# Free time behind list-scheduled operations and a new opening for a one-core transformer block

## The chip, the cores and the metric

The kernel runs on one core of a Trainium2 chip. A core has four compute engines that the profile names PE (TensorE, matrix products), DVE (VectorE), ACT (ScalarE) and POOL (GpSimd), and SP (SyncE), which issues most DMA transfers. Each engine takes its instructions in the order in which the program lists them; an instruction that waits for a semaphore holds everything behind it on its engine. The metric is device time in microseconds. Three runs of the kernel before took 972.73 to 976.04 us, with a median of 974.53.

## The reference

The kernel computes one transformer block with adaptive layer norm for a sequence of 2048 tokens of width 512. A conditioning vector gives six vectors of 512 (scale, shift and gate for each half of the block). Attention has 32 heads of 16 and a causal sliding window of 256; the FFN is SwiGLU with 1792 hidden units. All data are 32-bit floats.

```python
mod = (_silu(c) @ w_mod).reshape(c.shape[0], 6, 1, -1)
sa, ca, ga, sb, cb, gb = (mod[:, 0], mod[:, 1], mod[:, 2], mod[:, 3], mod[:, 4], mod[:, 5])
h = _layernorm(x, axis=-1) * (1 + ca) + sa
x = x + ga * _A_ref(h, A_wqkv, A_wo)          # windowed attention and out-projection
h = _layernorm(x, axis=-1) * (1 + cb) + sb
x = x + gb * _B_ref(h, B_w1, B_w3, B_w2)      # w2 (silu(w1 h) * (w3 h))
```

## The kernel before

A product in 32-bit precision is made from parts: an operand is split into a rounded part of type fp32r and the rest (a copy with rounding, and a subtraction), and three matmuls of 512 columns add up high by high, low by high and high by low. So a copy and a subtraction stand in front of nearly every matrix product: `wvh` and `wvl` for the value weights, `wq` (two parts) for the query and key weights, `hT` (two parts) for the normed and transposed input, `wo` and `o` for the out-projection, `w` for the FFN weights, `b` for FFN inputs.

The work falls into three stretches.

The opening (to about 90 us) loads x, the modulation weights and the value weights, makes rows of the modulation (`modulation`: four matmuls `row` on PE, a copy `out` to ACT, a turn into columns `turn` on PE, and `end` on DVE, which writes `modc`), the statistics and the normalization of the first 512 tokens (`ln1`: statistics on DVE, the power on POOL, `ln_apply` on DVE, transposes on PE, then for each of four 128-wide slices an ACT copy `h` with scale and shift, and the pair of DVE operations in `mod_split` that writes `hT`), the value products (`values`, tile `st`) and the first query and key products (`unit_a`, tile `pj`). Each function hands its operations with a time to `at(t, fn)`; they are sorted by that time and issued in this order. The times are offsets in the dictionaries W (opening) and Y (first units). They are a planner's units of order, not measured times. Before, a few set-up operations stood outside this list: masks and identity copies on DVE, the copy `sc32` of the conditioning vector, and the first `ring_fill`, which puts constants into the buffers (`ring`) of queries and keys; the fills of the other three token blocks were in the list, and POOL did them.

Attention runs as 32 units, 8 groups of four heads by 4 blocks of 512 tokens. A unit has a part a (query and key products, `pj`, with splitting), a part b (row maxima: score matmuls `mx` on PE, then a DVE operation L507 with the mask that leaves the maximum `mt`, then `mr` and a small matmul L522), and a part c (scores `st` again, exp on ACT to `pt`, window selects on POOL (L778) or DVE, products with the values `po`, L726). The order of these operations is written out by hand in the dictionary X.

From the last third of the units on, a list scheduler, class `Sched`, puts other work between the unit operations: loading and splitting of wo and of the FFN weights (`split`, L962 copy and L963 subtraction), the reciprocals of the softmax sums (L1065), the attention outputs multiplied by the reciprocals and split (`o_part`: L1095, L1087, L1090), the out-projection with the residual (`o_proj`, matmuls L1107, DVE L978), the second layer norm (L983 to L1003, L1228), its transposes (L1242) and splitting (L1246 to L1267), and the whole FFN. The FFN's block products are formed from sums and differences of blocks, seven products instead of eight, so DVE and POOL also form sums of tiles. The unit operations enter as `fixed`, with a time and an engine. `deal` goes forward in planned time: for each engine it takes the first operation by key whose inputs are ready, or else the one that is ready first, and picks the earliest over all engines; a fixed operation goes in when its time has come. Keys, and for many operations the engine, stand in the dictionary K; CAPS limits how many PSUM banks each use may hold.

Of the kernel before, what the change touches and what calls it, by code (L numbers as in the profile page):

```python
# [18 lines left out]
P = 128  # L19
# [24 lines left out]
W = dict(m=0.15, s=0.1, a=0.32, t=0.541, p=0.377, vs=1.762, vo=0.422, wq=-2.02, ws=-0.376, wv0=-1.811, wv=0.3, wvk=0.474, h0=0.539, h=6, hb=6.874, ls=3.287, la=1.146, rf=7.313, v=2, vt=1.75, m0=1.5, mt=0.7, ml=0.241, A=1.268, At=7.876, B=9.889)  # L44
# [22 lines left out]
CAPS = dict(tp=4, up=5, dn=5)  # L67
# [47 lines left out]
class Sched:  # L115
# [38 lines left out]
    def deal(self):  # L154
# [8 lines left out]
        order, self.dealt = [], []  # L163

# [102 lines left out]
LATE = 2.0  # L267

# [5 lines left out]
def us(t):  # L274
# [15 lines left out]
K = dict(be=(('POOL', 'POOL'), ('POOL', 'DVE'), ('POOL', 'POOL'), ('DVE', 'POOL'), ('POOL',  # L290
         'POOL'), ('POOL', 'DVE'), ('POOL', 'POOL')), hr=1.228, de=-0.011, wo=0.363, x1=5.427,
         xb=-11.259, xl=0.182, os=0.09, ol=(-29.26, -4.358, -61.448, -4.772), pl=(23.674, -19.281,
         -2.126, -37.597), pe=(1.308, 32.004, -0.229, 9.552), o=(-92.491, -1.503, 76.848, -7.065),
         n=(1, 1, 2, 2), w0=0.298, l2=0.646, f=3.115, fl=5.405, by=((('POOL', 'POOL'), ('POOL',
         'POOL'), ('DVE', 'DVE'), ('POOL', 'POOL')), (('POOL', 'POOL'), ('POOL', 'DVE'), ('DVE',
         'DVE'), ('POOL', 'POOL')), (('POOL', 'DVE'), ('DVE', 'DVE'), ('DVE', 'DVE'), ('DVE',
         'DVE')), (('POOL', 'POOL'), ('DVE', 'DVE'), ('DVE', 'DVE'), ('DVE', 'POOL'))), w=0.25,
         dn=1.72, ds=0.103, l3=-4.114, sw=('POOL', 'DVE', 'DVE', 'POOL'), su=(('POOL', 'DVE',
         'DVE', 'POOL'), ('POOL', 'POOL', 'POOL', 'DVE'), ('DVE', 'DVE', 'DVE', 'POOL')),
         sr=(('POOL', 'DVE', 'DVE', 'DVE', 'POOL', 'DVE', 'DVE', 'DVE', 'DVE', 'DVE', 'DVE'),  # L300
         ('POOL', 'DVE', 'POOL', 'DVE', 'POOL', 'DVE', 'DVE', 'POOL', 'DVE', 'POOL', 'POOL')))
@with_exitstack
def block_kernel(ctx: ExitStack, tc: tile.TileContext, x, wqk, wv, wo, w13, w2, c, wmod, out):
# [13 lines left out]
    for hh in range(2):  # L317
        r = slice(64 * hh, 64 * hh + 64)
        nc.vector.tensor_reduce(
            out=odd[r], in_=ident[r].rearrange("p (c o) -> p c o", o=4)[:, :, 2 - 2 * hh:4 - 2 * hh],  # L320
            op=ALU.add, axis=mybir.AxisListType.XY)
# [85 lines left out]
    nc.vector.tensor_scalar(later, mskk[:, 0], 0.0, None, op0=ALU.is_lt)  # L407
    mskr = ap.tile([P, 2, P], F32R, name="mskr")
    nc.vector.tensor_copy(mskr, mskk)
    mskk = mskr.bitcast(F32)  # L410
    identr = ap.tile([P, P], F32R, name="identr")
    nc.vector.tensor_copy(identr, ident)

    def ring_fill(b):
        for hh in range(2):
            k = ring.bitcast(F32)[:, 2 - 2 * hh, :, b * BT:(b + 1) * BT]
            eng = nc.vector if b == 0 and hh == 0 else nc.gpsimd
            eng.memset(k[:NM] if hh == 0 else k[:NS], 0.0)
            if hh:
                eng.memset(k[NS:NM], 1.0)  # L420
            eng.memset(k[NS:NS + 2], 1.0 - hh)
# [3 lines left out]
    def load_wqk(g, n):  # L425
# [144 lines left out]
    nc.vector.tensor_copy(sc32, sc[:, :, None].to_broadcast([P, KC, 32]))  # L570

    def modulation(j, s, t0, at):
# [14 lines left out]
        def out():  # L587
            v["e"] = p0.tile([P, D], F32, name="h32", bufs=3)
            nc.scalar.activation(v["e"], v[0], AF.Copy)
# [19 lines left out]
        for n, fn in enumerate((row, out, turn, end)):  # L609
            at(t0 + W["m"] * n, fn)  # L610

# [3 lines left out]
    def load_wv(k, n):  # L615
# [3 lines left out]
        elif n == 1:  # L619
            nc.scalar.activation(wvh[:, k], raw, AF.Copy)  # L620
        else:
            nc.gpsimd.tensor_tensor(out=wvl[:, k], in0=raw, in1=wvh.bitcast(F32)[:, k],
                                    op=ALU.subtract)
# [59 lines left out]
    ring_fill(0)  # L683
    h0 = -40.0
    modulation(0, 2, h0 - 1, at)
    modulation(1, 1, h0 - 0.9, at)
    for n in range(3):
        at(h0 + (W["wq"] if n == 0 else W["ws"] + n * 0.02), lambda n=n: load_wqk(0, n))
# [13 lines left out]
    m0 = v0 + W["vt"] * W["m0"]  # L702
    for n, (j, s) in enumerate(((3, 2), (4, 1), (2, 2), (5, 1))):
        t = v0 + W["vt"] * (W["m0"] + W["mt"] * n)
        at(h0 + W["ml"] if n < 2 else t - 2 * W["vt"] * W["mt"] + W["m"] * 0.5, lambda j=j, s=s: load_mod(j, s, nc.sync))
        modulation(j, s, t, at)
    at(v0 + W["vt"] * (W["m0"] + W["mt"] * 3) + 3.1 * W["m"], ones)
    for u in range(3):
        unit_a(u, h0 + W["A"] + W["At"] * u, at, Y)
# [891 lines left out]
```

## Time and profile before

| | before |
|---|---|
| median of three runs | 974.53 us (972.73 to 976.04) |
| profiled execution | 973.01 us |
| its span, first to last instruction | 971.3 us |
| mean granted TensorE clock | 0.99 |
| PE busy | 940.5 us |
| DVE, ACT, POOL busy | 743.1, 556.4, 542.8 us |

The profiled execution is one of its own; it lies 1.52 us below the median of the three. In rows of the trace the first number is the start, the second the time from the first start to the last end of a run of equal instructions, then engine, source line, operation, the tile written and the tiles read. Brackets at the end give the idle time of the engine before the row, and what released it. Half a clock means that a matmul of the same size takes twice as long. PE takes weights (PEld) ahead of the matmul that uses them. Rows can be shown overlapping, since the matmuls are pipelined and other engines start the next operation before the last has wholly ended.

### The profile page before, as it was taken

To read this page: it belongs to the slowest core of one execution; us is meant where nothing else is said; L and a number is where in the kernel's file an instruction comes from. 1 tells how busy PE (TensorE), PEld (TensorE's weight loads), DVE (VectorE), ACT (ScalarE), POOL (GpSimd) and SP (SyncE) were. 2 spreads that over 40 slices of the span, in tenths; PEclk is the share of its full clock that TensorE was granted. 3 is DMA by queue.
4 is the path that set the end of the run, shared out by engine and by line. 5 is a ranking of instruction groups with operands and counts; after the bars stand their busy time and mean duration, and the time that the engine had idled before them with its cause. 6 is when DMAs were issued, how large, how long until landed. Compare 5 with 4: busy or idle time off the path is not lost.

```text
span 971.3 us, 17147 instructions
## 1 busy us (share of the span) xinstructions
PE 940.5 (97%) x5316; PEld 716.7 (74%) x5316; DVE 743.1 (77%) x2032; ACT 556.4 (57%) x1252; POOL 542.8 (56%) x742
## 2 busy tenths in 40 slices
PE   5999999999999999998898999999999999999998
PEld 3578777777777776774577888888887888888886
DVE  7776799899989898999378686656679765677545
ACT  3433787787878787876578843433456343423330
POOL 7441787877777776765556765347759332222320
PEclk9999999999999999999799999999999999999999
DMA  8521354444454444335695564467654432222102
GB/s 294 182 88 34 118 175 153 143 160 139 146 178 143 144 144 143 133 122 180 211 237 145 188 225 149 142 206 249 188 199 166 141 119 89 69 62 75 44 23 87
DMA packets 80672, 141.65 MB, mean 146 GB/s; under 512 B 9538, under 2 KB 22338, under 8 KB 80580
## 3 DMA queue, kind: packets, MB, share of 16 engines
q1 hardware_dynamic: 79860, 139.50, 44.6%
q10 hardware_dynamic: 720, 1.05, 0.3%
q8 instruction: 42, 0.69, 0.3%
q14 instruction: 50, 0.41, 0.1%
HBM read 85.72 MB, written 34.61 MB: 124 GB/s over the span
## 4 chain that ended last, share of the span: by engine, by line
PE 83%; POOL 5%; DVE 5%; DMA 2%; issue 2%; ACT 1%; SPq 1%; POOLq 0%; DVEq 0%; ACTq 0%
PE st L1371 13%; PE mx L1371 11%; PE mx L500 7%; PE pj L447 7%; PE mx L1465 7%; PE st L750 7%; PE st L1465 7%; PE po L726 6%; PE pj L1371 5%; PE st L664 3%; PE pj L1465 2%; PE mx L1107 2%; POOL pt L778 2%; PE st L1107 2%; POOL qk L465 1%
## 5 line engine op out<-in xcount | busy, mean ns | idle before, releaser
L507 DVE CUSTOM_DVE_ANT_0 junk<-mx,mskq 128x384 bf16<-128x384 f32 (+2 forms) x512 | 256.2, 527 | 27.0 <-PE mx L500 25.5
L500 PE MATMUL mx<-ring 96*128 96x384 f32 (+2 forms) x512 | 154.9, 341 | 4.9 <-DVE mt L507 2.4
L750 PE MATMUL st<-ring 100*128 100x384 f32 (+2 forms) x512 | 155.7, 346 | 2.1 <-ACT pt L771 1.2
L778 POOL TENSOR_SCALAR_AFFINE_SELECT pt<-pt 128x256 f32<-128x256 f32 x268 | 109.3, 410 | 62.8 <-ACT pt L771 52.4
L447 PE MATMUL pj<-hT,wq 128*128 128x512 f32 x384 | 136.5, 405 | 1.2 <-DVE hT L364 1.2
L500 PEld LDWEIGHTS mx<-ring 96*128 96x128 f32 x512 | 93.5, 189 | 38.4 <-DVE mt L507 26.3
L771 ACT ACTIVATE pt<-st 128x256 f32<-128x256 f32 x268 | 96.2, 386 | 42.5 <-DVE st L768 34.9
L750 PEld LDWEIGHTS st<-ring 100*128 100x128 f32 x512 | 96.0, 191 | 23.0 <-issue 8.3
L726 PE MATMUL po<-pt,vS 128*17 128x384 f32 (+2 forms) x1408 | 97.7, 394 | 3.2 <-POOL pt L778 2.9
L963 POOL TENSOR_TENSOR w<-w,w 128x512 fp32r<-128x512 f32 (+2 forms) x36 | 59.8, 1678 | 62.1 <-ACT w L962 44.6
L1415 POOL TENSOR_TENSOR t<-t,t 128x512 f32<-128x512 f32 x28 | 39.7, 1416 | 96.1 <-DVE t L1403 94.4
L465 POOL TENSOR_TENSOR qk<-qkr,qk 128x512 fp32r<-128x512 f32 x64 | 82.8, 1294 | 15.9 <-ACT qkr L453 15.6
L768 DVE COPY_PREDICATED st<-later,st 128x128 f32<-128x128 uint8 x268 | 72.2, 291 | 17.1 <-PE st L750 13.7
L447 PEld LDWEIGHTS pj<-hT,wq 128*128 128x128 f32 x384 | 71.8, 190 | 8.2 <-DVE hT L364 1.5
L726 PEld LDWEIGHTS po<-pt,vS 128*17 128x17 f32 x1408 | 33.1, 98 | 49.5 <-issue 22.0
L1371 PE MATMUL st<-b,w 128*128 128x512 f32 x258 | 64.1, 390 | 0.0
L762 ACT ACTIVATE pt<-st 128x384 f32<-128x384 f32 (+2 forms) x128 | 52.9, 434 | 19.4 <-DVE st L758 12.3
L1403 DVE TENSOR_TENSOR t<-st,t 128x512 f32<-128x512 f32 x52 | 35.7, 687 | 36.4 <-PE st L1371 31.2
L795 POOL TENSOR_SCALAR_AFFINE_SELECT sm<-sm 128x256 f32<-128x256 f32 x109 | 42.1, 409 | 27.5 <-ACT sm L785 23.6
L1443 ACT ACTIVATE wq<-g 128x512 fp32r<-128x512 f32 x28 | 17.7, 634 | 67.9 <-PE st L1465 40.6
L1371 PE MATMUL mx<-b,w 128*128 128x512 f32 x222 | 56.0, 390 | 0.0
L1371 PEld LDWEIGHTS st<-b,w 128*128 128x128 f32 x258 | 48.4, 188 | 10.2
(270 smaller groups left out, 2093.4 us busy)
## 6 DMA issues: line engine op xcount, KB each, us to landing
ring<-qk SPq DMA_DIRECT2D x192, 128.0 KB
o_dr<-os SPq DMA_DIRECT2D x32, 256.0 KB
w<-wsum SPq DMA_DIRECT2D x14, 512.0 KB
w<-w2g SPq DMA_DIRECT2D x14, 512.0 KB
jb<-in_w SPq DMA_DIRECT2D x24, 256.0 KB
wraw<-in_w SPq DMA_DIRECT2D x7, 768.0 KB
w<-wraw SPq DMA_DIRECT2D x14, 384.0 KB
vS<-in_wmod SPq DMA_DIRECT2D x20, 256.0 KB
```

The lines of the kernel that those rows point to most:

```text
L447: nc.tensor.matmul(v["ps"], WQ[g][w][:, n // 3], hTp(i, n // 3, b * BT, BT), start=(n == 0), stop=(n == 3 * KC - 1))
L465: nc.gpsimd.tensor_tensor(out=v[n], in0=v["raw"], in1=v[1].bitcast(F32), op=ALU.subtract)
L500: nc.tensor.matmul(v[i][:, :n], queries(NS, a, gq, 1), keys(NS, hh, a, k0, gq + 1 - k0), start=True, stop=True)
L507: nc.vector.tensor_tensor_reduce(out=junk[:, :n], in0=v[i][:, :n], in1=mskq[:, 3 * P - n:], scale=1.0, scalar=-3e38, op0=ALU.add, op1=ALU. ...
L726: nc.tensor.matmul(po[32 * i:32 * i + DH + 1, qb * P:(qb + nq) * P], vS[:, kb, 4 * g + i], pts[i // 2][:, i % 2, c0:c0 + nq], start=first, ...
L750: nc.tensor.matmul(ps[:, :nq], keys(NM, hh, a, kb, 1), queries(NM, a, kb, nq), start=True, stop=not plus)
L768: nc.vector.copy_predicated(ps[:, 0], later, ps[:, 2])
L771: nc.scalar.activation(held[u, j, a][:, hh, :2], v[j, a, hh][:, :2], AF.Exp, scale=SCALE)
L778: nc.gpsimd.affine_select(out=pt[:, :, 2 * m], in_=pt[:, :, 0], **w)
L963: sch.op(eng, lambda: on_eng(eng).tensor_tensor(out=lo(), in0=src(), in1=hi().bitcast(F32), op=ALU.subtract), tt(eng, n), key, kl + kh, kl ...
L1371: nc.tensor.matmul(ps(bk), WT[s, n][w][:, col], BB[t, k][r], start=start and c == 0, stop=stop and c == 5, skip_group_check=True)
L1465: nc.tensor.matmul(ps(bk), tiles[hk + (h,)][:, i * P:(i + 1) * P], w2_of(last, y, f), start=(m == 0), stop=(m == 5))
```

## The change

Three things are changed at once.

In the scheduler, `coming` keeps the start times of the unit operations still to come on DVE, ACT and POOL. An operation with a key of zero or more that would end more than FIT = 0.3 after the start of the next unit operation on its engine is put behind that start. While units run, an operation on another engine that uses a result made by DVE, ACT or POOL or loaded by DMA gets its earliest time moved by SLACK: 0.5, or 2.5 after a transfer, if it is on DVE, ACT or POOL. The cap of PSUM banks for transposes goes from 4 to 2. The arithmetic of the scheduled operations is the same, and so are the 1,913 unit matmuls and their order.

The dictionary K is set anew: nearly all keys, and the engine for many sums and subtractions. The key offset `w` of weight loads goes from 0.25 to 22.056.

In the opening, the set-up operations become list entries and all ring fills go to POOL. The first block's and half of the second block's fills stand early, the rest in front of the first `values`. The value weights' subtractions are POOL's for the first slice and DVE's for the other three (`wp=1`); the first wq subtraction is DVE's. The value weights are loaded before those for queries and keys, ACT rounds them before it makes `h`, the copy `out` of a modulation row is done in two halves, and the modulation rows of the second norm (3 and 4) are loaded, and the first of them multiplied, earlier. Unit 0's part a starts a little later in the list (A0 = 2.1 for 1.268), the first part b too (B = 10.4 for 9.889).

```diff
-CAPS = dict(tp=4, up=5, dn=5)
+CAPS = dict(tp=2, up=5, dn=5)
...
+        coming = {e: [f[0] for f in fixed if f[2] == e] for e in ("DVE", "ACT", "POOL")}
+        over = max(f[0] for f in fixed)
...
+                    if key >= 0 and coming.get(e) and max(s, t) + o.occ > coming[e][0] + FIT:
+
+                        s = max(s, coming[e][0] + 0.01)
                     if s <= t:
...
                 t, fn, e, occ = fixed.pop(0)
+                if e in coming:
+                    coming[e].pop(0)
...
                 m = PEM if u.eng == "PE" and o.eng in ("ACT", "DVE", "POOL") else 0.0
+                if u.eng in coming and u.eng != o.eng and s < over:
+                    m += SLACK[1 if o.kb else 0]
...
+SLACK = (0.5, 2.5)
+FIT = 0.3
...
-    def ring_fill(b):
-        for hh in range(2):
-            k = ring.bitcast(F32)[:, 2 - 2 * hh, :, b * BT:(b + 1) * BT]
-            eng = nc.vector if b == 0 and hh == 0 else nc.gpsimd
...
+    def ring_fill(b, hh):
+        k = ring.bitcast(F32)[:, 2 - 2 * hh, :, b * BT:(b + 1) * BT]
+        nc.gpsimd.memset(k[:NM] if hh == 0 else k[:NS], 0.0)
+        if hh:
+            nc.gpsimd.memset(k[NS:NM], 1.0)
+        nc.gpsimd.memset(k[NS:NS + 2], 1.0 - hh)
...
-            nc.gpsimd.tensor_tensor(out=WQ[g][1], in0=WQ[g][2], in1=WQ[g][0].bitcast(F32),
-                                    op=ALU.subtract)
+            eng = nc.gpsimd if g else nc.vector
+            eng.tensor_tensor(out=WQ[g][1], in0=WQ[g][2], in1=WQ[g][0].bitcast(F32), op=ALU.subtract)
...
-            nc.scalar.activation(v["e"], v[0], AF.Copy)
+            for n in range(2):
+                nc.scalar.activation(v["e"][:, n * 256:n * 256 + 256], v[0][:, n * 256:n * 256 + 256], AF.Copy)
...
-            nc.gpsimd.tensor_tensor(out=wvl[:, k], in0=raw, in1=wvh.bitcast(F32)[:, k],
-                                    op=ALU.subtract)
+            eng = nc.gpsimd if k < W["wp"] else nc.vector
+            eng.tensor_tensor(out=wvl[:, k], in0=raw, in1=wvh.bitcast(F32)[:, k], op=ALU.subtract)
...
+    at(h0 - 9, fill_masks)
+    for n in range(2):
+        at(h0 - 9 + 0.1 * n, lambda n=n: ring_fill(0, n))
+    at(h0 - 8.7, lambda: ring_fill(1, 0))
+    at(h0 - 3 + 1.5 * W["s"], fill_sc)
+    at(h0 - 3 + 1.6 * W["s"], fill_odd)
...
     for k in range(KC):
-        for n in range(3):
-            at(h0 + (W["wv0"] if n == 0 else W["wv"] + 0.02 * n) + W["wvk"] * k * (n > 0),
-               lambda k=k, n=n: load_wv(k, n))
+        at(h0 + W["wv0"], lambda k=k: load_wv(k, 0))
+        at(h0 + W["wvh"][k], lambda k=k: load_wv(k, 1))
+        at(h0 + W["wvl"][k], lambda k=k: load_wv(k, 2))
...
-        at(h - W["rf"], lambda b=b: ring_fill(b))
+        for n in range(2):
+            if b > 1 or n:
+                at(h0 + W["rf"][b - 1], lambda b=b, n=n: ring_fill(b, n))
```

More of the change, by code (lines that the diff above doesn't have):

```diff
@@ L289 @@
       (("POOL", "DVE"),) * 3 + (("DVE", "DVE"),), (("POOL", "POOL"),) * 4)
[L290 to L301, printed above, removed]
+K = dict(be=(('DVE', 'POOL'), ('POOL', 'DVE'), ('POOL', 'POOL'), ('POOL', 'POOL'), ('POOL',
+         'POOL'), ('POOL', 'DVE'), ('POOL', 'POOL')), hr=-0.509, de=0.973, wo=-0.008, x1=3.03,
+         xb=-10.581, xl=-0.321, os=0.889, ol=(-5.644, 2.542, -7.922, -9.93), pl=(59.662, -1.998,
+         -17.346, -4.151), pe=(-4.742, -1.261, -1.181, 5.9), o=(-8.297, 1.854, 41.659, 8.586),
+         n=(1, 1, 2, 2), w0=0.564, l2=-0.214, f=1.179, fl=5.404, by=((('POOL', 'POOL'), ('POOL',
+         'POOL'), ('POOL', 'DVE'), ('DVE', 'DVE')), (('POOL', 'DVE'), ('POOL', 'DVE'), ('DVE',
+         'POOL'), ('POOL', 'POOL')), (('POOL', 'DVE'), ('DVE', 'POOL'), ('POOL', 'DVE'), ('DVE',
+         'DVE')), (('POOL', 'DVE'), ('DVE', 'DVE'), ('DVE', 'DVE'), ('DVE', 'DVE'))), w=22.056,
+         dn=1.202, ds=0.071, l3=-5.554, sw=('POOL', 'DVE', 'DVE', 'POOL'), su=(('POOL', 'POOL',
+         'DVE', 'POOL'), ('POOL', 'DVE', 'DVE', 'POOL'), ('DVE', 'DVE', 'POOL', 'DVE')),
+         sr=(('POOL', 'DVE', 'DVE', 'DVE', 'POOL', 'DVE', 'DVE', 'POOL', 'POOL', 'DVE', 'DVE'),
+         ('DVE', 'POOL', 'DVE', 'DVE', 'DVE', 'DVE', 'DVE', 'POOL', 'POOL', 'POOL', 'POOL')))
 @with_exitstack
@@ L315, in block_kernel, with fill_odd @@
     odd = cst.tile([P, 1], F32, name="odd")
-    for hh in range(2):
[L318 to L321, printed above, removed]
+    def fill_odd():
+        for hh in range(2):
+            r = slice(64 * hh, 64 * hh + 64)
+            nc.vector.tensor_reduce(
+                out=odd[r], in_=ident[r].rearrange("p (c o) -> p c o", o=4)[:, :, 2 - 2 * hh:4 - 2 * hh],
+                op=ALU.add, axis=mybir.AxisListType.XY)
+        nc.vector.tensor_copy(identr, ident)
     modc = cst.tile([P, 4, KC], F32, name="modc")
@@ L406, in block_kernel, with fill_masks @@
     later = ap.tile([P, P], mybir.dt.uint8, name="later")
-    nc.vector.tensor_scalar(later, mskk[:, 0], 0.0, None, op0=ALU.is_lt)
     mskr = ap.tile([P, 2, P], F32R, name="mskr")
-    nc.vector.tensor_copy(mskr, mskk)
+    identr = ap.tile([P, P], F32R, name="identr")
+    def fill_masks():
+        nc.vector.tensor_copy(mskr, mskw[:, :2])
+        nc.vector.tensor_scalar(later, mskw[:, 0], 0.0, None, op0=ALU.is_lt)
     mskk = mskr.bitcast(F32)
-    identr = ap.tile([P, P], F32R, name="identr")
-    nc.vector.tensor_copy(identr, ident)
-    def ring_fill(b):
-        for hh in range(2):
-            k = ring.bitcast(F32)[:, 2 - 2 * hh, :, b * BT:(b + 1) * BT]
-            eng = nc.vector if b == 0 and hh == 0 else nc.gpsimd
[L418 to L421, printed above, removed]
+    def ring_fill(b, hh):
[4 more added lines that the diff above has]
+        nc.gpsimd.memset(k[NS:NS + 2], 1.0 - hh)
     WQ = {}
@@ L609, in modulation @@
         for n, fn in enumerate((row, out, turn, end)):
-            at(t0 + W["m"] * n, fn)
+            at(h0 + W["mr"][j // 3] if n == 0 and j in (0, 3) else t0 + W["m"] * n, fn)
     wvh = p0.tile([P, KC, D], F32R, name="wvh")
```

18 lines of the change are left out of this document (8 added, 10 removed).

## The prediction, made before the changed kernel had run

> **What bounds the kernel now.** I read the page first (busy shares, and the chain that ended last), then busy time by stretches of the span, then the waits and the order of time in the two stretches where TensorE is not full. From the page:
>
> ```profile
> PE 940.5 (97%) x5316; PEld 716.7 (74%) x5316; DVE 743.1 (77%) x2032; ACT 556.4 (57%) x1252; POOL 542.8 (56%) x742
> PE 83%; POOL 5%; DVE 5%; DMA 2%; issue 2%; ACT 1%; SPq 1%; POOLq 0%; DVEq 0%; ACTq 0%
> ```
>
> PE is busy 97% of the span and carries 83% of the chain. Where it is not full is seen by stretches. The columns are length, busy PE, PEld, DVE, ACT, POOL (with counts), granted clock, DMA share, GB/s:
>
> ```profile
> 0.00:20.00 20.00, 10.68 (x51) 5.26 (x52) 13.99 (x27) 6.77 (x12) 14.41 (x26) 1.00 0.83 277
> 20.00:40.00 20.00, 18.58 (x94) 11.41 (x92) 17.00 (x23) 6.70 (x12) 14.25 (x12) 0.91 0.66 217
> 440.00:460.00 20.00, 17.02 (x130) 10.42 (x128) 18.32 (x68) 12.46 (x34) 9.08 (x19) 1.00 0.64 199
> 460.00:484.40 24.40, 20.46 (x124) 11.43 (x124) 8.53 (x23) 13.49 (x34) 12.90 (x18) 0.79 0.68 206
> 484.40:520.00 35.60, 35.60 (x189) 28.94 (x190) 25.07 (x47) 26.99 (x52) 21.04 (x15) 1.00 0.93 244
> 520.00:527.00 7.00, 4.26 (x17) 3.26 (x16) 6.93 (x12) 6.89 (x13) 3.34 (x3) 0.76 0.34 113
> 540.00:971.00 431.00, 427.56 (x1864) 346.80 (x1862) 289.75 (x379) 178.94 (x277) 187.67 (x157) 1.00 0.41 135
> ```
>
> Idle PE time is 9.3 us before 20, 1.4 in 20 to 40, 3.0 in 440 to 460, 3.9 in 460 to 484.4, 2.7 in 520 to 527. The clock adds to it: 0.91, 0.79 and 0.76 there, 1.00 elsewhere. From 100 to 440 the change moves nothing on PE, and from 540 on PE idles 3.4 of 431, mostly the end itself. So only the opening and the transition from attention to out-projection can pay.
>
> **The clock first, because both parts use it.** The same view, in stretches of 3.2 us:
>
> ```profile
> 17.50:20.80 3.30, 1.94 (x9) 0.94 (x7) 3.27 (x3) 3.30 (x7) 3.22 (x4) 1.00 1.04 395
> 21.00:24.20 3.20, 2.94 (x7) 1.61 (x7) 3.17 (x3) 0.29 (x1) 3.20 (x3) 0.50 1.02 367
> 457.80:461.10 3.30, 0.97 (x11) 0.43 (x10) 2.94 (x9) 1.76 (x4) 1.69 (x4) 1.00 0.71 201
> 461.30:464.50 3.20, 2.56 (x12) 1.99 (x16) 1.88 (x5) 2.13 (x7) 1.99 (x4) 0.50 0.01 3
> 464.80:467.90 3.10, 3.10 (x23) 1.32 (x16) 0.00 (x0) 0.79 (x2) 1.09 (x3) 0.50 0.55 188
> ```
>
> A stretch in which PE was busy 1.94 or 0.97 us is followed by one at half clock, and that one ends when PE was nearly full in it. The stretches lie 3.41 us apart (20.9, 24.3, 27.7, 31.1). [...]
>
> **Part 1, the opening.** Before, on DVE, POOL and ACT (start, length):
>
> ```profile
> 3.31 0.95 POOL L418 MEMSET ring<- 96x1024 f32 x1
> 11.89 2.29 POOL L421 MEMSET ring<- 2x1024 f32 x2
> 18.93 6.27 POOL L622 TENSOR_TENSOR wvl<-vS,wvh 128x512 fp32r<-128x512 f32 x4
> 3.79 0.69 DVE L349 BATCH_NORM_STATS2 bst<-xt 128x6 f32<-128x512 f32 x1
> 13.21 1.25 DVE L354 TENSOR_SCALAR xt<-xt,mv,rs0r 128x512 f32<-128x512 f32 x1
> 15.12 0.54 DVE L354 TENSOR_SCALAR xt<-xt,mv,rs0r 128x512 f32<-128x512 f32 x1
> 15.93 0.16 DVE L606 TENSOR_SCALAR modc<-mx 128x4 f32<-128x4 f32 x1 [0.28 <-PE mx L597]
> 24.09 1.65 DVE L364 TENSOR_TENSOR hT<-h,hT 128x512 fp32r<-128x512 f32 x1
> 25.66 0.41 DVE L363 CAST hT<-h 128x512 fp32r<-128x512 f32 x1
> 26.11 0.69 DVE L364 TENSOR_TENSOR hT<-h,hT 128x512 fp32r<-128x512 f32 x1
> 13.98 0.60 ACT L589 ACTIVATE h<-mx 128x512 f32<-128x512 f32 x1 [1.27 <-PE mx L584]
> 16.43 0.78 ACT L361 ACTIVATE h<-st,modc 128x512 f32<-128x512 f32 x1 [1.33 <-PE st L642]
> 20.66 0.64 ACT L620 ACTIVATE wvh<-vS 128x512 fp32r<-128x512 f32 x1
> 25.80 0.50 PE L664 MATMUL st<-wvh,hT 128*128 128x512 f32 x1 [0.84 <-DVE hT L364]
> ```
>
> The hT pairs (cast, subtraction) take 0.41 and 0.69 alone, and the subtraction 1.65 beside POOL's subtractions. PE waits on that chain and is dense from 25.80. The change removes POOL's wq subtraction and three of four wvl subtractions, and puts all four on DVE: 4 x 0.65 (pitch of a 0.69 subtraction) = 2.6 us more on the engine that PE waits for. The masks, identity and ring memsets only change place and engine before 10.5 us, in idle time of POOL ahead of the first statistics; nothing there is on the path, since the modulation rows wait for DMA. The two half copies of the modulation row are worth 0.3 at most on that path, which the applies and transposes share; I take 0.
>
> In the changed order ACT does four wvh copies first, then the four h (eight at the 0.60 pitch of 16.43 to 20.66, from 14.58): h0 ends at 17.6, h3 at 19.5. DVE is free at 16.1: wvl1 beside POOL's wvl0 ends at 17.7 (1.65), wvl2 and wvl3 at 19.0. Then come four hT pairs and, last, the wq subtraction, on which the ninth-oldest matmul of the block waits on the in-order PE. All this time POOL runs eight memsets of blocks 1 and 2, 16.6 to about 26, that stood elsewhere before. Their effect on DVE is the unknown. The rows: an apply beside memsets takes 1.25, alone 0.54 (mean pitch beside them 1.17, so +0.63); a statistics op beside a memset (3.79 and 3.31) takes 0.69, what the 512-column subtraction takes alone. No row has a subtraction beside a memset. Lower end, nothing lengthened: four pairs at 1.1, hT done 23.0 with h3 in time, wq at 23.6. Upper end, casts at 1.04 and subtractions at 1.32: pairs of 2.36, cut short when the memsets end, wq at 28.6. I take the casts lengthened and the subtractions not, since a memset reads no operand and the one-operand statistics row is undisturbed: pairs of 1.6, hT at 25.4, wq at 25.9. [...]
>
> So PE turns dense at 25.9 instead of 25.8 (+0.1). By then 8 matmuls of the block are done instead of 18, 10 x 0.24 (a 512-column matmul at full clock, the row of twelve in Part 3) = +2.4; four modulation matmuls pulled ahead save 1.0. The stretch 20.9 to 24.3 is at half clock and holds under two thirds of work, so 24.3 to 27.7 is at half too, where before it was full: (27.7 - 25.9)/2 = +0.9. Opening: 0.1 + 1.4 + 0.9 = +2.4. Ends: 23.6 - 25.8 + 1.4 + 0.3 (half clock to 24.3) = -0.5, and 28.6 - 25.8 + 1.4 + 1.3 (half clock to 31.1) = +5.5. The memsets leave the place where they also stood beside block 1's applies (32 to 36 us); PE reaches those transposes at about 40, so no gain. PE's later waits on DVE's maxima, near 67 and 72, I leave as they are.
>
> **Part 2, the transition.** Rows of DVE, POOL and PE:
>
> ```profile
> 454.33 0.88 DVE L1065 RECIPROCAL mT<-mT 32x128 f32<-32x128 f32 x1
> 458.09 0.95 DVE L1065 RECIPROCAL wqr<-wqr 96x128 f32<-96x128 f32 x1 [0.72 <-DMA wqr<-o_dr]
> 456.93 1.28 POOL L963 TENSOR_TENSOR wo<-wo,wo 128x512 fp32r<-128x512 f32 x1 [4.11 <-ACT wo L962]
> 455.69 0.92 PE L500 MATMUL mx<-ring 96*128 96x384 f32 x2 [0.95 <-DVE mt L507]
> 459.11 0.41 PE L726 MATMUL po<-pt,vS 128*17 128x128 f32 x8 [1.30 <-POOL pt L778]
> 461.94 0.40 PE L522 MATMUL mx<-ident,mr 128*32 128x128 f32 x1 [1.88 <-DVE mr L516]
> 471.42 1.29 POOL L1095 TENSOR_TENSOR qk<-qk,qk 128x512 f32<-128x512 f32 x1
> 473.95 0.41 PE L726 MATMUL po<-pt,vS 128*17 128x128 f32 x8 [0.38 <-POOL pt L778]
> ```
>
> Each PE wait has another stage's op ahead of the unit's op: reciprocals before L507, the wo subtraction (1.28) before the selects of 458.16. The changed order puts the wo copies and subtraction behind the unit's exps and selects, and one reciprocal behind the last row maximum with its 0.95 + 0.72 of DMA wait; two reciprocals (1.82 together) stay ahead of three L507, so the 0.95 wait stays. Of the 1.30 + 1.88 that can go I take 1.9: with po earlier, the next late thing is the last maximum: L507 three times (527 ns each, the mean of its group in the page) and the two small operations on mr, behind those reciprocals. The nine projection matmuls inside the last unit move behind it; 9 x 0.24 = 2.2 is only moved, and the wait of 0.38 and a small part of the clock loss go: 0.7. Clock: 457.8 to 461.1 would no longer be 0.97 busy, and the work done at half clock in 461.3 to 467.9 (2.56 + 3.10) could cost 2.8 less; I take half, 1.4. Sum -4.0. Ends: 0 (every wait is replaced by the next chain) and -6.4 (1.30 + 1.88 + 0.38, and the whole 2.8).
>
> **Part 3, second norm and FFN.** The norm of the second half starts at the end of its projections and ends in the PE turn (ACT and PE rows):
>
> ```profile
> 503.50 2.88 PE L1107 MATMUL pj<-wo,x1b 128*128 128x512 f32 x12
> 513.07 2.94 ACT L1228 ACTIVATE g<-x1a,nbB,rsB 128x512 f32<-128x512 f32 x4
> 516.89 0.60 PE L1242 MATMUL st<-ident,g 128*128 128x128 f32 x4
> 523.12 2.93 PE L1107 MATMUL st<-wo,o 128*128 128x512 f32 x6 [2.74 <-ACT t L1246]
> ```
>
> From 506.4 to the last g copy (516.0) are 9.7 us, covered by 45 matmuls (10.4 us). In the changed order 27 stand there, 6.2 us: a new wait of about 3.4, and half a stretch of clock, 1.4. The wait of 2.74 at 523.12 and its half clock (7.0 us at 0.76 hold 1.7) have the 18 matmuls as cover then and go. I take 0, ends -3 and +4. In the FFN the banks' cap, load keys and engines of sums change; PE idles nowhere there and the tail of the load queue is nearly the same: 0, ends 0 and +3.
>
> **Sum.** 973.0 (profiled execution; the median, 974.5, is 1.5 above) + 2.4 - 4.0 + 0 = 971.4, that is 1.6 below its own execution and 3.1 below the median.
>
> **Rivals.** (a) Forecast: casts alone lengthened, transition gains 4: 971.4; 968 to 974. (b) The opening's contention is full (subtractions too, wq at 28.6): +5.5 in Part 1, the rest as forecast: 974.5, no change. For it: the row of 1.65; against: POOL read an operand then. (c) Slower: POOL now has three multiplications of attention outputs by the reciprocals, which wait for DMA, and one subtraction (L1121, L1116 of the changed kernel) between the selects of the last two waves of probabilities; in order, at 1.29 each (POOL's row of 471.42), they hold the last selects, the po matmuls and PE for up to 5.2, and the stretch behind is at half clock (1.6): 971.4 + 6.8 = 978.2. It ends slower (above 977.4) from 6.0 on, clock included. For it: one such multiplication cost the 0.38 of 473.95; against: three exps on ACT come between.
> (d) The transition gains nothing because what it moves away comes back as the next chain's wait, opening +2.4: 975.4, against the median no change. (e) Opening undisturbed and all waits gone: 973.0 - 0.5 - 6.4 = 966.1.
>
> **Chances.** (a) 0.38, (b) 0.17, (c) 0.18, (d) 0.13, (e) 0.14. 0.3% of 974.5, about what a measurement tells from no change, is 2.9 us: faster is below 971.6, slower above 977.4. The edge of faster runs through the middle of (a), so I split it: 0.22 faster, 0.10 same, 0.06 slower. With (e) all faster, (c) and a third of (b) and (d) slower by the upper bounds of Part 3: faster 0.40, same 0.26, slower 0.34. The range 964 to 980 leaves out the far ends of (c) and (e), under 2 in 10; (a) alone is 968 to 974.
>
> **What would show it.** DVE's wq subtraction near 25.9 (23.6 or 28.6 by the ends), subtractions near 0.69 beside memsets, casts near 1.04; PE dense after it; granted clock half from 20.9 to 27.7. No PE wait for L778's successor or the last maximum at 459 to 462, clock above 0.79 in 460 to 484. PE waits about 3 us at the first turn of the second norm and not 16 matmuls later. PE full from 540 on. Wrong would be: DVE late after 28, or PE waits of over 1 us in the FFN.

## The result, and the profile after

The changed kernel took 978.8 us (median of 7 runs, 977.47 to 981.16) against 974.33 (972.73 to 976.04, 7 runs): a ratio of 1.0049 with a 95% interval of 1.0035 to 1.0062. It is slower by about 4.8 us, where 3.1 us faster had been forecast. The profiled execution of the changed kernel is its slowest run, 981.16 us, and that of the kernel before, 973.01, lies below its median; the two traces are therefore 8.1 us apart, 3.4 more than the ratio says.

The busy shares on the page of the changed kernel:

```profile
span 979.4 us, 17139 instructions
PE 949.0 (97%) x5316; PEld 721.4 (74%) x5316; DVE 728.3 (74%) x2034; ACT 555.9 (57%) x1258; POOL 525.5 (54%) x740
```

And the same stretches of it as in the prediction (length, PE, PEld, DVE, ACT, POOL, clock, DMA share, GB/s):

```profile
0.00:20.00 20.00, 12.32 (x55) 5.18 (x56) 13.16 (x29) 7.75 (x15) 15.38 (x28) 1.00 0.90 316
20.00:40.00 20.00, 19.40 (x98) 12.63 (x97) 10.01 (x25) 7.12 (x16) 5.53 (x6) 1.00 0.61 201
440.00:460.00 20.00, 17.67 (x133) 10.50 (x135) 16.88 (x63) 12.06 (x33) 7.58 (x18) 0.95 0.64 194
460.00:484.40 24.40, 21.91 (x118) 13.34 (x116) 7.09 (x18) 12.70 (x32) 15.21 (x19) 0.64 0.69 202
484.40:520.00 35.60, 31.66 (x150) 23.29 (x150) 22.32 (x41) 23.05 (x43) 21.56 (x14) 0.98 0.87 224
527.00:540.00 13.00, 10.88 (x41) 8.45 (x40) 12.83 (x25) 8.35 (x17) 4.87 (x4) 0.87 0.01 3
```

Three things are to be seen. The opening is better: PE is busier in both stretches, and from 20 to 40 nothing is at half clock (0.91 before). From 100 to 440 the same unit matmul stands 1.7 to 2.6 us earlier than before, and 2.1 at the end of that stretch. From 460 to 484.4 PE is busier than before (21.91 for 20.46), but at a clock of 0.64 for 0.79. And from 484.4 to 520, where PE had been busy for the whole 35.60, it idles 3.9 us, and 2.1 more from 527 to 540. The last projection stands 7.4 us later than before, with six FFN matmuls ahead of it in both kernels, and the last matmul of all 8.1 us later; so the FFN carries only 0.7 us of this execution. In the kernel before the six are this row (in the changed kernel, five stand at 528.48 and one at 531.92):

```profile
530.50 1.55 PE L1371 MATMUL st<-b,w 128*128 128x512 f32 x6
```

The opening of the changed kernel on DVE, POOL and PE:

```profile
15.55 2.32 DVE L643 TENSOR_TENSOR wvl<-vS,wvh 128x512 fp32r<-128x512 f32 x3
20.11 0.52 DVE L380 CAST hT<-h 128x512 fp32r<-128x512 f32 x1
20.67 0.69 DVE L381 TENSOR_TENSOR hT<-h,hT 128x512 fp32r<-128x512 f32 x1
21.28 0.53 DVE L380 CAST hT<-h 128x512 fp32r<-128x512 f32 x1
21.85 0.69 DVE L381 TENSOR_TENSOR hT<-h,hT 128x512 fp32r<-128x512 f32 x1
22.46 0.68 DVE L453 TENSOR_TENSOR wq<-wqr,wq 128x512 fp32r<-128x512 f32 x1
19.24 1.12 POOL L435 MEMSET ring<- 100x1024 f32 x1
20.42 1.11 POOL L438 MEMSET ring<- 2x1024 f32 x1
17.63 3.04 PE L603 MATMUL mx<-vS,sc 128*32 128x512 f32 x8
20.60 0.50 PE L684 MATMUL st<-wvh,hT 128*128 128x512 f32 x1
23.20 0.49 PE L464 MATMUL pj<-hT,wq 128*128 128x512 f32 x1 [0.47 <-DVE wq L453]
```

Beside memsets a subtraction takes 0.69, as alone. A cast takes 0.52 for 0.41 alone, and the memset beside it is longer too (1.11 for 0.95). The cast of 20.11 started while the memset of 19.24 ran and ended 0.28 us after it; the memset of 20.42 started while that cast ran. An hT pair follows the other after 1.17 us, and the wq subtraction ends at 23.1. PE is busy until 20.60 with one row of the modulation, whose four products (eight in the trace) take 3.04 us as their data arrive by DMA (ahead of three of them PEld waits 0.52 to 0.53 us for `in_wmod`); then it waits only 0.47, for wq.

The larger of PE's waits between 452 and 548:

```profile
457.12 0.28 PE L539 MATMUL mx<-ident,mr 128*32 128x128 f32 x1 [1.31 <-DVE mr L533]
470.90 0.44 PE L776 MATMUL st<-ring 100*128 100x384 f32 x1 [0.40 <-ACT pt L797]
475.04 1.47 PE L752 MATMUL po<-pt,vS 128*17 128x384 f32 x8 [1.63 <-POOL pt L804]
509.79 3.15 PE L1133 MATMUL mx<-wo,o 128*128 128x512 f32 x12 [0.40 <-POOL o L1116]
513.96 1.88 PE L1133 MATMUL mx<-wo,o 128*128 128x512 f32 x7 [1.01 <-DVE o L1116]
517.08 0.33 PE L1268 MATMUL st<-ident,g 128*128 128x128 f32 x1 [0.56 <-ACT g L1254]
531.92 0.50 PE L1397 MATMUL st<-b,w 128*128 128x512 f32 x1 [2.12 <-DVE b L1293]
```

The wait of 1.30 for the selects at 459.11 is gone, and the 0.95 before the row maxima; the 1.88 at 461.94 is 1.31 at 457.12. At 470.90 the changed kernel stands 5.85 us ahead of the same matmul before (476.75): 2.1 from the opening and 3.75 from the transition. Six projection matmuls, 1.4 us of work, had run by then in the kernel before and come later now, so that the transition has won about 2.35. The lead is then lost, from this place on:

```profile
469.16 1.28 POOL L1121 TENSOR_TENSOR qkr<-qkr,qk 128x512 f32<-128x512 f32 x1
470.40 1.28 POOL L1121 TENSOR_TENSOR qk<-qk,qk 128x512 f32<-128x512 f32 x1
471.64 1.29 POOL L1121 TENSOR_TENSOR wq<-wq,wq 128x512 f32<-128x512 f32 x1
472.88 1.27 POOL L1116 TENSOR_TENSOR o<-qkr,o 128x512 fp32r<-128x512 f32 x1
474.10 0.89 POOL L804 TENSOR_SCALAR_AFFINE_SELECT pt<-pt 128x256 f32<-128x256 f32 x2
```

The selects come behind four operations of the out-projection, 5 us, and PE waits 1.63. What follows is dearer than the wait. PE stretches of 3.2 to 3.3 us, with the granted clock as the third number from the end; the first row is from an earlier place, behind the wait of 1.31:

```profile
458.10:461.30 3.20, 3.00 (x25) 1.63 (x27) 0.52 (x2) 2.94 (x8) 2.83 (x5) 0.50 0.34 112
471.70:474.90 3.20, 1.71 (x19) 0.83 (x19) 0.30 (x1) 2.51 (x6) 3.13 (x4) 1.00 0.89 246
475.10:478.40 3.30, 3.18 (x14) 1.44 (x14) 0.91 (x3) 0.77 (x2) 1.89 (x3) 0.50 0.51 148
478.50:481.80 3.30, 3.19 (x11) 2.61 (x12) 0.88 (x3) 1.90 (x6) 1.49 (x1) 0.50 0.58 161
481.90:485.10 3.20, 3.20 (x10) 2.52 (x9) 0.83 (x3) 0.28 (x1) 1.28 (x1) 0.50 0.29 75
485.30:488.50 3.20, 3.20 (x17) 2.22 (x20) 2.04 (x5) 0.00 (x0) 0.00 (x0) 0.99 0.31 87
```

After a stretch with 1.71 us of work, three stretches run at half clock although PE is 96% to 100% busy in them. Nearly 10 us of work costs double, the nine projection matmuls among it (4.15 us from 479.98, where twelve take 2.89 at full clock from 542.04; before, the nine had run between the last unit's matmuls). The last score matmul (L776) starts at 483.92, for 484.60 before; of the lead of 5.85 us 0.67 is left. At the projections of 486.79, for 486.88 before, it is 0.09, with the same work done in both kernels. From there to the last projection another 7.5 us are lost.

How long the clock stays at half differs from one execution to the next. Run e9 below has the same instructions in the same order up to 526 us, and its trace the same two waits (1.32 for 1.31, and 1.61 for 1.63). Behind the first it has full clock throughout, where the changed kernel's trace is at half from 458.0 to 468.3; behind the second it has 6.8 us at half, not 10.2. There the last products with the values stand 4.0 us ahead of the kernel before, here 0.08. So what the two waits cost in the median can't be read from this one trace.

### The profile page after: what moved, and what is told of

Its sections match the earlier page's. It is cut to its first block, busy times and chain, and to the rows that moved or that the text cites. A ratio compares the mean times of both kernels' runs of the same rounds, so it can differ in the third digit from the quotient of the medians.

```text
span 979.4 us, 17139 instructions
## 1 busy us (share of the span) xinstructions
PE 949.0 (97%) x5316; PEld 721.4 (74%) x5316; DVE 728.3 (74%) x2034; ACT 555.9 (57%) x1258; POOL 525.5 (54%) x740
## 4 chain that ended last, share of the span: by engine, by line
PE 81%; DVE 6%; POOL 5%; issue 3%; DMA 3%; ACT 2%; SPq 0%; POOLq 0%; DVEq 0%; ACTq 0%
PE mx L1397 12%; PE st L1397 11%; PE st L1491 8%; PE pj L464 8%; PE st L776 8%; PE mx L517 8%; PE po L752 7%; PE mx L1491 5%; PE st L684 3%; PE pj L1397 3%; PE pj L1491 3%; POOL pt L804 2%; POOL qk L482 1%; DVE junk L524 1%; PE st L1133 1%
## 5 line engine op out<-in xcount | busy, mean ns | idle before, releaser
L776 PE MATMUL st<-ring 100*128 100x384 f32 (+2 forms) x512 | 158.3, 351 | 1.9 <-ACT pt L797 1.2
L776 PEld LDWEIGHTS st<-ring 100*128 100x128 f32 x512 | 97.2, 193 | 24.8 <-issue 9.0
L989 POOL TENSOR_TENSOR w<-w,w 128x512 fp32r<-128x512 f32 (+2 forms) x37 | 54.8, 1488 | 77.4 <-ACT w L988 77.4
L1397 PE MATMUL mx<-b,w 128*128 128x512 f32 x252 | 62.9, 390 | 0.0
L1429 DVE TENSOR_TENSOR t<-st,t 128x512 f32<-128x512 f32 x47 | 32.4, 689 | 40.2 <-PE st L1397 32.1
L1429 DVE TENSOR_TENSOR t<-mx,t 128x512 f32<-128x512 f32 x52 | 35.9, 690 | 35.2 <-PE mx L1397 27.3
```

The source lines that it names most:

```text
L776: nc.tensor.matmul(ps[:, :nq], keys(NM, hh, a, kb, 1), queries(NM, a, kb, nq), start=True, stop=not plus)
L1397: nc.tensor.matmul(ps(bk), WT[s, n][w][:, col], BB[t, k][r], start=start and c == 0, stop=stop and c == 5, skip_group_check=True)
L1429: return nc.vector.tensor_add(o, x, y)
```

## The experiments

Each run is given by its median, by its ratio to the kernel before on the same chip with a 95% interval, and by the difference in us that this ratio makes of 974. Traces are of one execution each.

**The parts apart.** First the new opening with the old scheduler and keys (e1), then the reverse (e2).

For e1, in the changed kernel:

```diff
-        coming = {e: [f[0] for f in fixed if f[2] == e] for e in ("DVE", "ACT", "POOL")}
...
-                    m += SLACK[1 if o.kb else 0]
...
-CAPS = dict(tp=2, up=5, dn=5)
+CAPS = dict(tp=4, up=5, dn=5)
-K = dict(be=(('DVE', 'POOL'), ...
+K = dict(be=(('POOL', 'POOL'), ...
```

> The new opening with the scheduler, the cap and the keys of before. By the trace of the changed kernel the opening is worth -2.1 us (every unit matmul from 100 to 440 us stands 2.0 to 2.2 earlier), so 972.2 if the rest does not answer to it. Rival: the units' end takes it back, 974.3. The unit order cannot differ, so the waits at 459.11 and 461.94 of the kernel before should stand again, 2.1 earlier.

Measured: 969.08 us, ratio 0.9955 (0.9942 to 0.9968), -4.4 us, twice what the changed kernel's trace had let expect. This is the fastest kernel of the study, ahead of both. The old waits stand again, 2.9 and 4.4 us earlier:

```profile
459.09 0.29 PE L527 MATMUL mx<-ident,mr 128*32 128x128 f32 x1 [1.57 <-DVE mr L521]
518.75 2.93 PE L1121 MATMUL st<-wo,o 128*128 128x512 f32 x6 [2.75 <-ACT t L1260]
```

The reverse (e2), in the kernel before:

```diff
+        coming = {e: [f[0] for f in fixed if f[2] == e] for e in ("DVE", "ACT", "POOL")}
...
+                    m += SLACK[1 if o.kb else 0]
...
-CAPS = dict(tp=4, up=5, dn=5)
+CAPS = dict(tp=2, up=5, dn=5)
-K = dict(be=(('POOL', 'POOL'), ...
+K = dict(be=(('DVE', 'POOL'), ...
```

> The new scheduler, cap and keys with the opening of before. If the two parts add, 978.8 + 2.1 = 980.9. Rival: the phase of the clock stretches decides what the later stalls cost, so that it comes out anywhere from 976 to 983.

Measured: 982.19 us, ratio 1.0089 (1.0064 to 1.0113), +8.7. So opening (-4.4) and scheduling (+8.7) add to +4.3, near the measured 4.8. The opening was a gain; the new schedule lost twice as much.

**The rule and the keys.** Both with the new opening. In e3 the new lines of `deal` stay, cap and keys are those of before:

```diff
-CAPS = dict(tp=2, up=5, dn=5)
+CAPS = dict(tp=4, up=5, dn=5)
...
-K = dict(be=(('DVE', 'POOL'), ...
+K = dict(be=(('POOL', 'POOL'), ...
```

> The new opening and the new rule of the scheduler with the keys and cap of before. Theory, the keys (the order after the units) cost the time: the waits at 459 and 462 go, the transposes of the second norm and the first FFN product stand as before, about 969 to 972. Rival, the rule itself costs it, since it puts ready work behind the units: 977 to 981, with PE waits between 470 and 545.

Measured: 979.06, ratio 1.0065 (1.0047 to 1.0082), +6.3, and 10.7 behind the opening alone.

The other way (e4), the new keys and cap with the old `deal`:

```diff
-        coming = {e: [f[0] for f in fixed if f[2] == e] for e in ("DVE", "ACT", "POOL")}
...
-                    if key >= 0 and coming.get(e) and max(s, t) + o.occ > coming[e][0] + FIT:
-                        s = max(s, coming[e][0] + 0.01)
...
-                    m += SLACK[1 if o.kb else 0]
```

> The new opening and the new keys and cap with the old rule. Theory, the keys cost the time: 977 to 981, with PE waiting at the turns of the second norm and before the first FFN product. Rival, the rule costs it: 970 to 973.

Measured: 977.25, ratio 1.0031 (1.0015 to 1.0046), +3.0, and 7.4 behind the opening alone. Each half alone costs about as much as both together (9.2). So neither is the cause by itself: the rule spoils the old order, and the keys spoil it without the rule. The cap, which came with the keys, was not tried alone. The largest wait of e4 is again at a select, here behind five of POOL's operations:

```profile
472.21 0.63 PE L740 MATMUL po<-pt,vS 128*17 128x128 f32 x8 [4.57 <-POOL pt L792]
```

**The two parts of the rule**, with the new opening and the old keys and cap. FIT alone (e5):

```diff
-SLACK = (0.5, 2.5)
+SLACK = (0.0, 0.0)
```

> New opening, old keys and cap, the new rule with FIT alone (SLACK 0). The rule with both cost 10.0 us against the opening alone (979.1 against 969.1). Theory S, the slack costs it, since it makes every step of the out-projection's chain later in the plan by 0.5 and each load by 2.5: about 971 here. Rival F, putting operations behind the units' next ones costs it: about 977 to 979. The waits at the reciprocals (459 to 462 before) should be shorter either way.

Measured: 973.16, ratio 0.9983 (0.9966 to 1.0000), -1.7: FIT alone costs about 2.7 of the opening's gain, less than the rival said and more than the theory. The wait for the last row maximum is 0.53, for 1.57 with the opening alone: shorter, as expected.

SLACK alone (e6):

```diff
-FIT = 0.3
+FIT = 1e6
```

> New opening, old keys and cap, the new rule with SLACK alone (FIT without effect). Theory S: 977 to 980, with PE waits between 500 and 545. Rival F: about 970.

Measured: 984.40, ratio 1.0095 (1.0070 to 1.0120), +9.3: 13.6 behind the opening alone. The slack carries the cost; with FIT beside it (e3) the time is 3 us less, though the intervals overlap. Its PE waits and a POOL row:

```profile
525.58 0.50 PE L1397 MATMUL mx<-b,w 128*128 128x512 f32 x1 [2.72 <-POOL b L1293]
533.57 2.93 PE L1397 MATMUL mx<-b,w 128*128 128x512 f32 x6 [7.49 <-ACT t L1432]
538.36 2.89 PE L1133 MATMUL pj<-wo,o 128*128 128x512 f32 x12
534.34 1.27 POOL L1116 TENSOR_TENSOR o<-qkr,o 128x512 fp32r<-128x512 f32 x1
```

With the opening alone 6 FFN matmuls stand ahead of the last 24 projection matmuls on PE, here 18 stand ahead of the last 48. While they wait, first for the second norm's split on POOL, then for L1432, which stands on ACT behind the norm's copies, 10.2 us go by, and the projections' last inputs are made behind the norm's (534.34). From 520 to 545 PE is busy 14.79 us there, against 24.98 with the opening alone.

The slack between engines alone (e12):

```diff
-SLACK = (0.5, 2.5)
+SLACK = (0.5, 0.0)
-FIT = 0.3
+FIT = 1e6
```

> New opening, old keys and cap, FIT without effect, SLACK of 0.5 between engines and none after a load. With both parts of the slack the time was 984.4. Theory, the 2.5 after a load are what makes the out-projection late: 969 to 972 here. Rival, the 0.5 per step adds up over the chain: 978 to 984.

Measured: 972.74, ratio 0.9983 (0.9970 to 0.9996), -1.7. The 0.5 between engines costs 2.7 against the opening alone; the other 11 us of the slack's 13.6 come with the 2.5 after a load (by difference; that part was not run alone).

**The changed kernel without slack (e7):**

```diff
-SLACK = (0.5, 2.5)
+SLACK = (0.0, 0.0)
```

> The changed kernel with SLACK 0. Theory S: the chain after the units comes earlier, 972 to 975. Rival, the new keys carry the cost by themselves, as they did with the old rule (977.3): 977 to 979.

Measured: 977.17, ratio 1.0035 (1.0020 to 1.0050), +3.4. With the new keys the slack matters little (4.8 with it, and the intervals overlap); the rival holds here. Without the slack PE waits 4.46 for a select behind five of POOL's operations, nearly as in e4; with it, 1.63 behind four. So the slack gains at that place and loses elsewhere.

**What POOL does beside the hT chain** (e8), with the new opening alone:

```diff
-wp=1,
+wp=4,
...
-            eng = nc.gpsimd if g else nc.vector
+            eng = nc.gpsimd
```

> The new opening alone, but with the four subtractions of wvl and wq back on POOL ahead of the ring memsets, where they read operands beside DVE's hT chain. If reading is what lengthens DVE's subtractions, hT pairs take about 3.1 instead of 1.17 while POOL subtracts (6 to 7 us) and PE turns dense 2 to 4 us later: 971 to 973 against 969.1. Rival: the order of ACT and of the modulation rows made the gain, then 969.

Measured: 971.12, ratio 0.9962 (0.9947 to 0.9978), -3.7 for -4.4, which the intervals do not separate. The trace tells more:

```profile
17.66 1.65 DVE L369 TENSOR_TENSOR hT<-h,hT 128x512 fp32r<-128x512 f32 x1
19.23 1.49 DVE L368 CAST hT<-h 128x512 fp32r<-128x512 f32 x1
21.37 2.42 DVE L368 CAST hT<-h 128x512 fp32r<-128x512 f32 x1
25.00 0.69 DVE L369 TENSOR_TENSOR hT<-h,hT 128x512 fp32r<-128x512 f32 x1
22.56 0.95 POOL L423 MEMSET ring<- 96x1024 f32 x1
23.56 1.12 POOL L425 MEMSET ring<- 4x1024 f32 x1
23.84 0.50 PE L672 MATMUL st<-wvh,hT 128*128 128x512 f32 x1 [0.68 <-DVE hT L368]
```

The subtraction of 17.66 takes 1.65 beside POOL's, that of 25.00 0.69 beside a memset, in one execution. That of 20.76, begun 0.04 us ahead of POOL's wq subtraction, takes 0.69, and POOL's 1.82. The hT chain ends at 25.7, for 22.7 with the opening alone, but PE's waits there are 0.72 and 0.68 for one of 0.80, and from 24.2 on its matmuls stand only 0.3 later. So the four subtractions are a small part of the opening's gain. The rest lies with its other edits (the order of the modulation rows and of ACT, the early memsets), which were not run apart.

**The late place of DVE and POOL** (e9), in the changed kernel, with the order kept:

```diff
+            def put(n):
+                return "DVE" if half == 0 and (k, n) in ((0, 4), (0, 7), (0, 8), (1, 1)) else e[n]
...
-                    (nc.gpsimd if eng == "POOL" else nc.vector).tensor_tensor(
+                    (nc.gpsimd if run == "POOL" else nc.vector).tensor_tensor(
```

> The changed kernel with the same order of operations, but four subtractions of the second norm (after the first) done by DVE in place of POOL. In the trace of the changed kernel DVE's operations from 525 to 532 take 1.75 to 1.79 each beside POOL's, alone 0.69, and PE waits 2.12 for one of them at 531.92, with the next stretch at half clock. Theory, the shared time of DVE and POOL bounds that place: DVE saves 4.3 and gains 2.8, the wait shrinks by 1.5 to 2.1 and the clock stretch goes: 975 to 977 against 978.8. Rival, ACT's chain bounds it: no change.

Measured: 976.20, ratio 1.0029 (1.0019 to 1.0040), +2.8, about 2 us less than the changed kernel (the intervals overlap between 1.0035 and 1.0040). The wait of 2.12 and its half-clock stretch are gone from the trace, as the theory said: the six FFN matmuls stand in a row, 1.55 us from 524.50. From the last products with the values to the last projection this trace loses 4.0 us against the kernel before, that of the changed kernel 7.5. In the changed kernel these rows stood there; alone, DVE's L1293 takes 0.69 (538.07):

```profile
526.71 1.78 DVE L1121 TENSOR_TENSOR qk<-qk,qk 128x512 f32<-128x512 f32 x1
528.41 1.77 DVE L1121 TENSOR_TENSOR wq<-wq,wq 128x512 f32<-128x512 f32 x1
530.11 1.75 DVE L1293 TENSOR_TENSOR b<-t,b 128x512 fp32r<-128x512 f32 x1
527.90 3.41 POOL L1285 TENSOR_TENSOR t<-t,t 128x512 f32<-128x512 f32 x2
```

**The selects put first** (e10), in the changed kernel: the order of the list changed at one place.

```diff
     order = sch.deal()
+    mult = [o for o in sch.dealt if o.eng == "POOL" and (o.tag or "")[:2] == ("op", 0)][0]
+    k = [i for i, f in enumerate(order) if f is mult.fn][0]
+    j = [i for i in range(k, len(order)) if unit.get(id(order[i])) == "POOL"][0]
+    moved = [f for f in order[k:j] if id(f) in dealt and (dealt[id(f)].tag or "")[:2] == ("op", 0)
+             and dealt[id(f)].eng != "SP"]
+    order = put(moved, order[j])
```

`dealt` and `unit` give the scheduler's and the units' operations of the order, and `put` takes the moved ones out and sets them behind the unit's selects `order[j]`.

> The changed kernel with one move in the order: the selects of the next wave of probabilities (and the exp in front of them) stand ahead of the three multiplications and the subtraction on POOL, not behind. Theory: the PE wait of 1.63 at 475.04 goes, and with it up to 10 us at half clock that follow: 974 to 977. Rival, the projections then wait for the multiplications instead: 978 to 980.

Measured: 979.86, ratio 1.0067 (1.0050 to 1.0084), +6.5: the time that the rival said, by another wait. The projections are not what waits; the wait of 1.63 has moved, not gone:

```profile
473.67 0.45 PE L776 MATMUL st<-ring 100*128 100x384 f32 x1 [2.76 <-ACT pt L788]
472.61 0.63 ACT L1113 ACTIVATE o<-qkr 128x512 fp32r<-128x512 f32 x1 [2.21 <-POOL qkr L1121]
```

ACT's copy of `o` now waits for POOL's later multiplication, with the unit's exps behind it on ACT.

Both edits together (e11), of e9 and e10:

> Both of these: 971 to 975 if they add; no better than the better of the two if the chain of the out-projection bounds the stretch from 470 to 540 as a whole.

Measured: 977.04, ratio 1.0038 (1.0023 to 1.0053), +3.7: no better than e9.

**Whether the opening's gain depends on where the clock's stretches fall.** In the trace of the opening alone its lead from 100 to 440 is 2.2 to 3.1 of the 4.4 us. With 5 (e13), and then 9 (e14) and 15 (e15) in place of 5, in the new opening alone:

```diff
+            if n == 0 and t < 5:
+                nc.tensor.matmul(v["ps"], hTp(w, k, t * P, P), i[:, k], start=True, stop=True)
```

> The new opening alone, with 5 value products' first matmul done twice (the first result is overwritten): about 1.15 us more PE work before 60 us, nothing else changed. Phase theory: the time moves by 1.15 plus or minus up to 2 us, by where the half-clock stretches fall. Rival, no phase: 969.1 + 1.15 = 970.2, less what later waits absorb.

> The same with 9, about 2.1 us, so that the units stand where they stood in the kernel before. Phase theory: the gain between 440 and 485 goes, 973 to 974. Rival: 971.2.

> The same with 15, about 3.45 us, one period of the clock's grid. Both theories: 969.1 + 3.4 = 972.5; with e14 above it, the phase theory stands.

Measured: 970.77, 971.27 and 972.90, ratios 0.9967 (0.9949 to 0.9984), 0.9968 (0.9949 to 0.9987) and 0.9985 (0.9967 to 1.0003), so -3.2, -3.1 and -1.5. The time follows the delay (about 1.2, 1.3 and 2.9 us later than without), with no step at 9 (by estimate 2.1 us, about two thirds of a stretch of 3.41). The rival's times come out, and nothing speaks for the phase theory: single executions of one kernel differ by up to 7 us here, but the medians do not hang on the offset. The test at 9 is weaker than meant, since in its trace the units from 100 to 440 still stand 1.1 to 2.1 us ahead of the kernel before. In the trace of the opening alone the lead grows from 2.5 to 5.0 us between 440 and 485, with 6.8 us at half clock there for 10.2 before, and ends at 4.4. Whether that is so in the median stays open.

## Why the prediction was wrong

**Opening, forecast +2.4, measured -4.4** (-2.1 in the profiled execution). Four terms failed.

The first is the effect of POOL's memsets on casts. I gave each cast the apply's +0.63, and it got +0.11. The applies had not been lengthened by a fixed amount: in the kernel before, each of the three beside memsets ended 0.28 us after the memset that ran when it started (12.11 and 11.83 for the first), so its length went with what was left of that memset. The applies stood back to back, each beside nearly a whole memset. Between two casts stands a subtraction, which took 0.69 beside the memsets, as alone, and while it ran most of the memset went by. The pairs came at 1.17 instead of 1.6, 1.7 us for four. The choice between the ends was right for subtractions (0.69 in the changed kernel's trace and in e8's).

The second is the start of that chain. The three wvl subtractions were done at 17.9, not 19.0: the first started at 15.55 for 16.1, and took 1.11 beside POOL's and not 1.65. Together the two terms put the end of wq at 23.1 for 25.9, below my lower end of 23.6. The modulation's column came 0.5 us earlier (15.47 for 15.93); that the half copies, which I had set at nothing, did this is not shown, since in e7, with the same opening, it came at 16.42.

The third is a count. By 25.8 the kernel before had done 13 matmuls of the block (five to `pj`, eight to `st`), not 18, so the matmuls left over are 5 x 0.24 = 1.2 and not 2.4. The fourth is the clock: no half-clock stretch followed, the +0.9 was not paid, and the one of before, 20.9 to 24.3, went too: PE was busy for all of the 3.41 us ahead of 20.9, before for 2.05 (60%). The two thirds in that term were my estimate, and no run shows them as a limit: in the kernel before half clock also followed 2.51 us of work in 3.41 (74%, up to 478.3), and in e9 full clock followed 2.08 (61%, up to 457.06).

With what was measured the sum is 23.2 - 25.8 + 1.2 - 1.0 = -2.4, and by 45 us the same work stood 2.2 us earlier.

**Transition, forecast -4.0, measured +2.0 in the profiled execution**, where the opening's lead of 2.1 had become 0.09 at its end. The waits up to 470.9 went as forecast, but the clock did not: I had put 1.4 less for it, and it stayed at half for 10.2 us from 458.0, for 6.8 before. The step that failed is that the rest of the unit would follow: rival (c) had the place (POOL's four operations ahead of the selects, 5.2 us) but made it a case of its own. The wait was 1.63; with the clock at half for 10.2 us after it, the lead was gone in this execution. I had priced a half-clock stretch at 1.6 and taken it to end after one.

**Second norm, forecast 0 (ends -3 and +4), measured +7.5 in the profiled execution.** This is the largest loss, beyond its upper end. From 484.4 to 540 PE's idle time grew from 2.7 to 6.1 us, with two half-clock stretches for one (1.7 more); the other 2.5 us are in time that counts as busy, as when transposes come one by one at 0.33 each, where four in a row take 0.60. A lead of 0.09 became a lag of 7.4. The new wait at the turn, which I had put at 3.4, was there with 2.5, in pieces of 0.38 to 0.56 behind ACT's copies; the old wait of 2.74 did go, as expected. But two others took its place: projections that wait for their inputs (0.40 and 1.01), and the first FFN product (2.12), which stands ahead of 48 projection matmuls, where before it stood ahead of 24 and did not wait. The step that failed is the cover: I had counted matmuls as cover but not asked whether their own inputs would be ready. After 520 DVE and POOL have seven of the out-projection's operations to do, for four before; they meet the second norm's there, and beside POOL's two-operand operations DVE's took 1.75 to 1.79 there, for 0.69 alone. e9 shows that share, about 2 us; e6 shows that the rule's slack can make such an order.

**FFN, forecast 0** (ends 0 and +3): 0.7 us in the profiled execution, within its ends.

**Rivals.** (c), 978.2, came nearest to the time and had the right place, but not the right terms: the wait was 1.63 for 5.2, the clock behind it cost about 4.8 (half of 9.57 us of work) for 1.6, and no rival had the second norm as its main loss. That the time lies within my range is luck: the opening's error and those of the other two had opposite signs. The split of the chances, added up, gives 0.36 faster, 0.30 same and 0.34 slower, not 0.40, 0.26 and 0.34.

What stays open: why the new keys with the old rule cost 7.4 us at several places at once, beyond the 4.57 shown; any change of a key moves the whole order, so one place can't be tried alone by keys. How the 9.2 us of the new schedule divide between transition and second norm in the median is open too, since the traces differ in their half-clock times.

## What to carry to other kernels

A list scheduler that delays work to protect what is urgent makes a debt: the delayed chain meets the next stage. Here a margin on every load made most of the rule's cost with the old keys (11 of 13.6 us, by difference), and little difference with the new ones, so a margin is to be timed with the order that it is used in. When work is moved behind, ask whether what counts as cover has its own inputs by then. And changes that come together should be timed apart: here the opening alone was 4.4 us faster, and the whole 4.8 slower.

## What the runs showed of the hardware that was not expected

A cast on DVE was longer beside a memset on POOL, and so was a memset that started beside a cast, though the rows overlap little (0.25 and 0.21 us at the cast of 20.11). In the changed kernel each of the four casts (17.80, 18.94, 20.11, 21.28) ended 0.28 us after the memset that ran when it started, and each next memset, which started while the cast ran, took 1.11 to 1.14 for 0.95. The casts took 0.50 to 0.53 for 0.41: most of each memset ran beside the subtraction of 0.69 between two casts. In e8 the cast of 21.37 started beside a subtraction of POOL's that ended at 22.6, and it ended at 23.8, 0.28 us after the memset of 22.56: 2.42 us for 0.41. What lies behind this no run shows.

Half clock did not always end after one busy stretch: from 475.1 to 485.1 three stretches with PE 96%, 97% and 100% busy stayed at half, and from 458.1 three with 94%, 100% and 100%. The matmuls in the first two of the stretches from 475.1 were small score products and products with 17 columns of weights in part; whether that is the reason no run here shows. The same order in e9 had no half clock at the first place and 6.8 us at the second.
